# ScalarE asks for the first weights beside SyncE's first tile of x, and the zeros for the passes without data are cleared in two parts

## The chip, the cores and the metric

The kernel runs on one core of a Trainium2 chip. Its engines are TensorE (PE, with its weight loads shown apart as PEld), VectorE (DVE), ScalarE (ACT), GpSimd (POOL) and SyncE (SP); 16 DMA engines serve the core, and SP, ACT and POOL can ask for transfers. The metric is the time of one execution on the device in microseconds (us); the kernel before is given by the median of three runs.

## The reference

The input x has 2048 tokens of 576 features, in float32. Three things are computed from it and mixed:

```
g = _sigmoid((x * gate_w).sum(-1, keepdims=True))
a = _A_ref(x, A_w_r, A_w_i)        # irfft2( rfft2(x) * (w_r + 1j*w_i) )
b = _B_ref(x, B_w_gate, B_w_up, B_w_down)
                                   # h = _gelu(x @ w_gate) * (x @ w_up);  h @ w_down
return g * a + (1 - g) * b
```

w_gate and w_up are 576 by 4608, w_down is 4608 by 576. Most of the work is in these three products.

## The kernel before, in words

Every product is made at nearly full float32 precision out of several passes of TensorE: an operand is split into a high and a low part (tile names ending in hi and lo), and the high-high, high-low and low-high products are added. A pass is one MATMUL of a 128x128 block of weights with up to 512 columns.

The hidden layer has 36 blocks of 128 features, the tokens are cut into two halves (p), and each half into two tiles of 512 tokens (tb). All instructions are written in a fixed order, engine by engine (a manual schedule); an engine executes its own list in order, and semaphores connect the lists. The queues of SP, ACT and POOL issue their transfers in list order too.

The change is at the very start. Contraction over the 576 features is done in five steps k (KT = 5): k = 0 to 3 are 128 features each, k = 4 is the last 64, laid twice. `first_chains` (its passes are line 881) writes the first accumulations: for k = 0, 1, 2, then 4 and 3, the passes of hidden block 0 (into the PSUM tiles px) and of hidden block 1 (into pgu). For a step k it takes

- x0[k], a tile of x (a slice of `til`, 128 by 512, 256 KB), loaded by SP at line 1442 or 1446;
- w0[:, k] and w1[:, k], the weights of hidden blocks 0 and 1 (slices of `low`, 128 by 256, 128 KB each: gate and up), loaded by SP at lines 1444 and 1448 for k = 0 to 2, and by POOL at line 1470 for k = 4 and 3.

ACT makes the high part of the weights (line 240, tile gub) and DVE the low part (line 1477, also gub). The high part of x0[0] is made by DVE (a CAST, line 1476, tile xhi), later ones by ACT (line 240), and the low part by DVE (line 1481, tile xlo).

Before this data is there, TensorE runs passes without data: DVE clears a tile `idle` (a slice of the tile hb, line 1461), and six passes multiply zeros by zeros (line 1467). A small ACTIVATE on a cleared column (`warm`, a slice of gate, line 1464) brings ACT's table load to this time. POOL then clears 16 columns of `idle` (line 1468), which makes it wait for the end of the passes without data, and only then asks for its four slices of weights.

SP's semaphores for transfers go round in a ring of eight: the ninth transfer is issued when the first has landed, and so on.

Of the kernel before, what the change touches and what calls it, by code (L numbers as in the profile page):

```python
# [15 lines left out]
P = 128  # L16
# [9 lines left out]
TB = 512  # L26
# [123 lines left out]
def _block_of_token():  # L150

    out = [0] * 16
    for o in range(16):
        out[4 * LEFT[o % 4] + LEFT[o // 4]] = o
    return out, [4 * TAKEN[o % 4] + TAKEN[o // 4] for o in out]
# [20 lines left out]
def _build(nc, tc, a):  # L176
    with ExitStack() as ctx:
# [3 lines left out]
        vec, act, pl, pe = nc.vector, nc.scalar, nc.gpsimd, nc.tensor  # L181
# [4 lines left out]
        def f(x):  # L186
            return x.bitcast(F32)
# [7 lines left out]
        _, loc = _block_of_token()  # L195
# [28 lines left out]
        def ps_gu():  # L224
            return psum.tile([P, TB], F32, name="pgu", tag="pgu", bufs=2)
# [1212 lines left out]
        x0 = [til[i // 9][:, TB * (i % 9):TB * (i % 9 + 1)] for i in range(2 * KT)]  # L1438
        w0, w1 = (raw[j][:, 0:KT * 256].rearrange("p (t k) -> p t k", t=KT) for j in range(2))
        w0d, w1d = (a["wgu"][j].rearrange("p (t k) -> p t k", t=KT) for j in range(2))  # L1440
        for k in (0, 1, 2, 3):
            nc.sync.dma_start(x0[k], a["xt"][0][:, k, 0:TB])
            if k < 3:
                nc.sync.dma_start(w0[:, k], w0d[:, k])
            if k == 2:
                nc.sync.dma_start(x0[4], a["xt"][0][:, 4, 0:TB])
            if k < 3:
                nc.sync.dma_start(w1[:, k], w1d[:, k])
            if k == 2:
                nc.sync.dma_start(msk, a["msk"])  # L1450
# [7 lines left out]
        load_xs(0, 1, [tmp[:, D + TB * q:D + TB * (q + 1)] for q in range(4)])  # L1458

        idle = hb[2][:, 0]  # L1460
        vec.memset(f(idle), 0.0)
        warm = gate[:, 0:1]
        vec.memset(warm, 0.0)
        act.activation(warm, warm, AF.Gelu_apprx_tanh)
        ps = ps_gu()
        for _ in range(6):
            pe.matmul(ps, idle[:, 0:P], idle, start=True, stop=True)
        pl.memset(f(idle)[:, 0:16], 0.0)
        for w, wd, k in ((w0, w0d, 4), (w0, w0d, 3), (w1, w1d, 4), (w1, w1d, 3)):
            pl.dma_start(w[:, k], wd[:, k])  # L1470
# [163 lines left out]
```

## Time and profile before

| what | us |
|---|---|
| median of three runs | 1324.69 |
| lowest and highest of the three | 1323.77 and 1325.9 |
| the profiled execution, whole | 1325.16 |
| its span, first to last instruction | 1323.4 |
| what lies around the span (1325.16 - 1323.4) | 1.76 |
| PE busy in the span | 1317.2 |
| DVE busy | 1163.2 |
| ACT busy | 871.8 |
| POOL busy | 274.5 |

Times inside the execution are microseconds from the start of the span. Durations of instructions come from this one profiled execution. A busy engine is one that has an instruction in flight: matmuls are pipelined, so a PE that is always busy may still do its passes at different paces.

### The profile page before, as it was taken

How to read it: one execution, taken by the hardware profiler on the slowest of the kernel's cores; microseconds unless marked ns; L12 is line 12 of the kernel's file. 1: busy time of each engine (PE TensorE's matmuls, PEld its weight loads, DVE VectorE, ACT ScalarE, POOL GpSimd, SP SyncE). 2: the span in 40 equal slices, each digit the busy share in tenths (PEclk: the TensorE clock that was granted, in tenths of full speed). 3: DMA queues.
4: the chain of work that ended last, by engine and by line, in shares of the span. 5: the costliest groups of instructions: out<-in, count | busy, mean ns of one | idle time of the engine just before them, and what ended most of it. 6: DMA issues, size and time to landing. Idle time of an engine off the chain costs nothing.

```text
span 1323.4 us, 20232 instructions
## 1 busy us (share of the span) xinstructions
PE 1317.2 (100%) x7294; PEld 1166.3 (88%) x7294; DVE 1163.2 (88%) x1654; ACT 871.8 (66%) x1583; POOL 274.5 (21%) x347
## 2 busy tenths in 40 slices
PE   9999999999999999999999999999999999999998
PEld 7888888888888888888888898888888888888888
DVE  7789999978999997976889889799999879999854
ACT  5676765665657557787688888547675676676562
POOL 0011121221212212122302231211222242222331
PEclk9999999999999999999999999999999999999999
DMA  9346776797677777999989998787777897766897
GB/s 352 139 116 130 131 135 136 158 267 167 146 153 139 151 156 183 278 237 280 284 251 247 219 210 206 124 279 194 153 150 148 202 232 163 135 141 131 182 195 181
DMA packets 109221, 247.57 MB, mean 187 GB/s; under 512 B 12864, under 2 KB 18624, under 8 KB 107328
## 3 DMA queue, kind: packets, MB, share of 16 engines
q0 software_dynamic: 46560, 96.82, 45.2%
q1 hardware_dynamic: 62128, 149.01, 34.1%
q8 instruction: 57, 0.93, 0.3%
q10 hardware_dynamic: 432, 0.44, 0.1%
q14 instruction: 44, 0.36, 0.1%
HBM read 133.88 MB, written 109.95 MB: 184 GB/s over the span
## 4 chain that ended last, share of the span: by engine, by line
PE 96%; DVE 2%; DMA 1%; ACT 0%; issue 0%; SPq 0%; DVEq 0%; ACTq 0%
PE pdn L945 33%; PE pgu L1292 20%; PE px L1292 20%; PE pgu L1294 3%; PE px L1294 3%; PE pgu L861 3%; PE pgu L862 3%; PE pgu L863 3%; DMA til<-away 1%; PE pdn L305 1%; PE px L305 1%; PE px L861 1%; PE px L862 1%; PE px L863 1%; PE pgu L867 1%; PE pgu L868 1%
## 5 line engine op out<-in xcount | busy, mean ns | idle before, releaser
L958 POOL DMA_DIRECT2D yd<-stg x264 | 227.0, 865 | 937.7 <-ACT stg L977 864.3
L977 ACT ACTIVATE stg<-pdn,omg 128x576 f32<-128x576 f32 x276 | 204.4, 742 | 318.1 <-PE pdn L945 197.2
L945 PE MATMUL pdn<-dn,hb 128*128 128x288 f32 x1572 | 230.3, 294 | 0.0
L945 PEld LDWEIGHTS pdn<-dn,hb 128*128 128x128 f32 x1572 | 221.5, 188 | 8.9 <-ACT stg L977 0.4
L1279 DVE TENSOR_TENSOR gub<-low,gub 128x768 fp32r<-128x768 f32 x124 | 118.2, 954 | 9.7 <-ACT gub L1276 7.3
L1292 PE MATMUL pgu<-xhi,gub 128*128 128x512 f32 x392 | 121.6, 392 | 0.0
L240 ACT ACTIVATE gub<-low 128x512 fp32r<-128x512 f32 (+2 forms) x147 | 97.8, 666 | 23.0 <-DVE low L1269 14.5
L945 PEld LDWEIGHTS pdn<-dn,ext 128*128 128x128 f32 x672 | 100.8, 188 | 8.0
L1292 PE MATMUL pgu<-til,gub 128*128 128x512 f32 x420 | 107.5, 391 | 0.0
L945 PE MATMUL pdn<-dn,gub 128*128 128x288 f32 x672 | 106.5, 294 | 0.0
L945 PE MATMUL pdn<-dn,ext 128*128 128x288 f32 x672 | 106.5, 294 | 0.0
L945 PEld LDWEIGHTS pdn<-dn,gub 128*128 128x128 f32 x672 | 95.0, 188 | 0.0
L1292 PEld LDWEIGHTS pgu<-til,gub 128*128 128x128 f32 x420 | 76.9, 188 | 14.8 <-DVE gub L1279 0.3
L1292 PE MATMUL px<-xhi,gub 128*128 128x512 f32 x280 | 86.9, 391 | 0.0
L1292 PE MATMUL px<-til,gub 128*128 128x512 f32 x336 | 85.8, 391 | 0.0
L945 PE MATMUL pdn<-dn,hx 128*128 128x288 f32 x516 | 81.7, 294 | 0.0
L1292 PEld LDWEIGHTS pgu<-xhi,gub 128*128 128x128 f32 x392 | 70.9, 188 | 12.1
L1269 DVE TENSOR_TENSOR low<-low 128x768 f32<-128x768 f32 x81 | 77.2, 954 | 0.8
L1292 PE MATMUL pgu<-xlo,gub 128*128 128x512 f32 x196 | 76.4, 390 | 0.0
L862 PE MATMUL pgu<-xhi,gub 128*128 128x512 f32 x188 | 73.7, 392 | 0.0
L861 PE MATMUL pgu<-xhi,gub 128*128 128x512 f32 x188 | 73.7, 392 | 0.0
L863 PE MATMUL pgu<-xlo,gub 128*128 128x512 f32 x188 | 73.3, 390 | 0.0
(274 smaller groups left out, 2966.6 us busy)
## 6 DMA issues: line engine op xcount, KB each, us to landing
yd<-stg POOLq DMA_DIRECT2D x264, 288.0 KB, 5.0
low<-ws SPq DMA_DIRECT2D x94, 384.0 KB, 4.8
gub<-wd SPq DMA_DIRECT2D x56, 288.0 KB, 3.9
low<-wgu SPq DMA_DIRECT2D x13, 640.0 KB, 8.6
rows<-col POOLq DMA_DIRECT2D x32, 256.0 KB, 6.4
gub<-ws SPq DMA_DIRECT2D x18, 384.0 KB, 5.3
lo<-dn SPq DMA_DIRECT2D x18, 288.0 KB, 2.9
dn<-lo POOLq DMA_DIRECT2D x18, 288.0 KB, 5.4
```

The costliest lines, as they stand in the source:

```text
L240: act.activation(o, i, AF.Copy)
L305: pe.matmul(v[al][:, :NK], c[:, al, q], two(x)[:, al], start=n == 0, stop=n == 2)
L861: pe.matmul(ps, w[:, 0, k, c], xhi[tb][:, k], start=k == 0, stop=False)
L862: pe.matmul(ps, w[:, 1, k, c], xhi[tb][:, k], start=False, stop=False)
L863: pe.matmul(ps, w[:, 0, k, c], xlo[tb][:, k], start=False, stop=False)
L945: pe.matmul(ps[half], h[:, l, c], d[:, q, half * HD:(half + 1) * HD], start=part == 0 and n == 0, stop=part == 1 and n == 2)
L958: pl.dma_start(yd[u], o, accum_op=ALU.add)
L977: at(n, lambda: put(u, lambda o: act.activation(o.rearrange("p (c k) -> p c k", c=2), v[:, :, 0:HD], AF.Copy, scale=omg[:, u:u + 1]), i == 0))
L1269: vec.tensor_tensor(o, p, q, ALU.subtract)
L1279: vec.tensor_tensor(w[:, 0:5:2], x, f(w[:, 1:4]), ALU.subtract)
L1292: pe.matmul(ps, l, x[:, t], start=first and t == 0 and q == 0, stop=False, skip_group_check=True)
L1294: pe.matmul(ps, w[:, 512 + P * s:512 + P * (s + 1)], xt, start=False, stop=True, skip_group_check=True)
```

## The change

Two edits, both in the first lines that are written for the engines.

First, ACT is given a transfer: w0[:, 0], the weights of hidden block 0 for k = 0, which SP issued as its second transfer. It is now the first entry on ACT's list, ahead of the table load. SP's later transfers each move up by one place.

Second, the tile of zeros is cleared by two instructions, the first 128 columns and then the other 384, and the passes without data are two of 128 columns (on the part cleared first) and five of 512, in place of six of 512.

```
@@ -1438,9 +1438,10 @@
         w0d, w1d = (a["wgu"][j].rearrange("p (t k) -> p t k", t=KT) for j in range(2))
+        act.dma_start(w0[:, 0], w0d[:, 0])
         for k in (0, 1, 2, 3):
             nc.sync.dma_start(x0[k], a["xt"][0][:, k, 0:TB])
-            if k < 3:
+            if 0 < k < 3:
                 nc.sync.dma_start(w0[:, k], w0d[:, k])
             if k == 2:
                 nc.sync.dma_start(x0[4], a["xt"][0][:, 4, 0:TB])
@@ -1458,13 +1459,14 @@
         idle = hb[2][:, 0]
-        vec.memset(f(idle), 0.0)
+        vec.memset(f(idle[:, 0:P]), 0.0)
+        vec.memset(f(idle[:, P:]), 0.0)
         warm = gate[:, 0:1]
         vec.memset(warm, 0.0)
         act.activation(warm, warm, AF.Gelu_apprx_tanh)
         ps = ps_gu()
-        for _ in range(6):
-            pe.matmul(ps, idle[:, 0:P], idle, start=True, stop=True)
+        for n in (P, P, TB, TB, TB, TB, TB):
+            pe.matmul(ps[:, 0:n], idle[:, 0:P], idle[:, 0:n], start=True, stop=True)
```

Lines behind the first edit have a number one higher in the changed kernel, and two or more behind the second. Apart from these rows and the numbering, the lists of the five engines are the same in both kernels, and so are their waits, save that the two first transfers have changed semaphores.

SP's list at its start, before (til is x, low is weights, wgu and xt are the tensors in DRAM):

```order
L1442 DMA til_69<-xt 128x512
L1444 DMA low<-wgu 128x256
L1448 DMA low<-wgu 128x256
L1442 DMA til_69<-xt 128x512
L1444 DMA low<-wgu 128x256
L1448 DMA low<-wgu 128x256
```

and in the changed kernel:

```order
L1443 DMA til_69<-xt 128x512
L1449 DMA low<-wgu 128x256
L1443 DMA til_69<-xt 128x512
L1445 DMA low<-wgu 128x256
L1449 DMA low<-wgu 128x256
L1443 DMA til_69<-xt 128x512
```

The second entry is gone: w1[:, 0] now follows x0[0] at once, and all behind it stands one place earlier.

ACT's list at its start, before (gate is the cleared column, gub the split weights):

```order
L1464 ACT_TABLE_LOAD
L1464 ACTIVATE gate<-gate 128x1
L240 ACTIVATE gub_71<-low 128x256
L240 ACTIVATE gub_72<-low 128x256
L240 ACTIVATE gub_71<-low 128x256
```

and in the changed kernel:

```order
L1441 DMA low<-wgu 128x256
L1466 ACT_TABLE_LOAD
L1466 ACTIVATE gate<-gate 128x1
L240 ACTIVATE gub_71<-low 128x256
L240 ACTIVATE gub_72<-low 128x256
```

One transfer stands ahead of the table load; the rest of ACT's list has not moved.

PE's list at its start, before:

```order
L1467 MATMUL pgu<-hb_82 128x512 x6
L881 MATMUL px_220<-xhi_63,gub_71 128x512
L881 MATMUL px_221<-xhi_63,gub_71 128x512
L881 MATMUL px_220<-xhi_63,gub_71 128x512
L881 MATMUL px_221<-xhi_63,gub_71 128x512
```

and in the changed kernel:

```order
L1469 MATMUL pgu<-hb_82 128x128 x2
L1469 MATMUL pgu<-hb_82 128x512 x5
L881 MATMUL px_222<-xhi_63,gub_71 128x512
L881 MATMUL px_223<-xhi_63,gub_71 128x512
L881 MATMUL px_222<-xhi_63,gub_71 128x512
```

Only the passes without data differ: 2 x 128 + 5 x 512 = 2816 columns in place of 6 x 512 = 3072.

## Rows read from the trace of the kernel before

**Rows 1.** The page: busy time by engine, and the chain that ended last, by engine.

```profile
PE 1317.2 (100%) x7294; PEld 1166.3 (88%) x7294; DVE 1163.2 (88%) x1654; ACT 871.8 (66%) x1583; POOL 274.5 (21%) x347
...
PE 96%; DVE 2%; DMA 1%; ACT 0%; issue 0%; SPq 0%; DVEq 0%; ACTq 0%
```

**Rows 2.** Waits of PE, whole span: waited for, us in total, times, longest.

```profile
PE pgu L1467 <- DVE gate L1463: 1.5, 1, 1.5
PE px L305 <- DVE rows L293: 0.7, 1, 0.7
```

**Rows 3.** The chain that ended last, 0 to 20 us: start, us, what.

```profile
1.45 2.93 PE pgu L1467 x6
4.38 2.39 PE px L881 x6
6.77 1.39 PE pgu L881 x6
8.16 1.36 PE px L881 x6
```

**Rows 4.** Timeline of PE in short windows: start, us (of all in the row), passes.

```profile
1.45 0.80 PE L1467 MATMUL pgu<-hb 128*128 128x512 f32 x1 [1.45 <-DVE gate L1463]
...
3.75 0.63 PE L1467 MATMUL pgu<-hb 128*128 128x512 f32 x1
4.37 0.79 PE L881 MATMUL px<-xhi,gub 128*128 128x512 f32 x1
...
5.39 0.92 PE L881 MATMUL px<-xhi,gub 128*128 128x512 f32 x2
...
5.82 0.49 PE L881 MATMUL px<-xhi,gub 128*128 128x512 f32 x1
6.15 0.63 PE L881 MATMUL px<-xlo,gub 128*128 128x512 f32 x2
```

**Rows 5.** Timeline of DVE and ACT, 0 to 4.4 us: what leads to the passes.

```profile
0.73 1.28 ACT L1464 ACT_TABLE_LOAD   x1 [0.73 <-PEq L1620]
...
0.92 0.48 DVE L1461 MEMSET hb<- 128x512 f32 x1 [0.92 <-PEq L1620]
1.35 0.06 DVE L1463 MEMSET gate<- 128x1 f32 x1
...
2.03 0.20 ACT L1464 ACTIVATE gate<-gate 128x1 f32<-128x1 f32 x1
...
3.60 0.43 DVE L1476 CAST xhi<-til 128x512 fp32r<-128x512 f32 x1 [2.19 <-DMA til<-xt]
3.90 0.42 ACT L240 ACTIVATE gub<-low 128x256 fp32r<-128x256 f32 x1 [1.67 <-DMA low<-wgu]
```

**Rows 6.** Timeline of SP, 0 to 14 us: issue of its transfers.

```profile
0.74 0.38 SPq L1442 DMA_DIRECT2D til<-xt  x1
1.18 0.42 SPq L1444 DMA_DIRECT2D low<-wgu  x1
1.64 0.43 SPq L1448 DMA_DIRECT2D low<-wgu  x1
2.12 0.43 SPq L1442 DMA_DIRECT2D til<-xt  x1
...
6.21 0.33 SPq L1442 DMA_DIRECT2D til<-xt  x1
```

**Rows 7.** Line 1012, the output's stores: ACT's issue of a transfer, ns min/median/max.

```profile
L1012 ACTq DMA_DIRECT2D y<-stg x3: 338/339/374, 1317.6 to 1320.4; - x3
```

**Rows 8.** DMA traffic from 1.7 to 3.3, 3.3 to 4.8 and 4.8 to 6.8.

```profile
DMA packets 287, 0.40 MB, mean 248 GB/s; under 512 B 27, under 2 KB 159, under 8 KB 287
...
DMA packets 175, 0.20 MB, mean 132 GB/s; under 512 B 18, under 2 KB 139, under 8 KB 175
...
DMA packets 546, 0.71 MB, mean 353 GB/s; under 512 B 60, under 2 KB 342, under 8 KB 546
```

**Rows 9.** Timeline, 4 to 14 us: POOL's start, and two operands with the passes behind them.

```profile
4.50 2.33 POOL L1470 DMA_DIRECT2D low<-wgu x4
...
6.88 0.62 ACT L240 ACTIVATE xhi<-til 128x512 fp32r<-128x512 f32 x1
...
7.77 0.88 PEld L881 LDWEIGHTS px<-xhi,gub 128*128 128x128 f32 x4
...
12.27 0.75 DVE L245 SCALAR_TENSOR_TENSOR xtl<-xtl,msk,til 128x512 fp32r<-128x512 f32 x1
...
13.22 0.87 PEld L881 LDWEIGHTS px<-xtl,gub 128*128 128x128 f32 x4
```

More of the change, by code (lines that the diff above doesn't have):

```diff
@@ L1440, in _build @@
         w0d, w1d = (a["wgu"][j].rearrange("p (t k) -> p t k", t=KT) for j in range(2))
+        act.dma_start(w0[:, 0], w0d[:, 0])
         for k in (0, 1, 2, 3):
             nc.sync.dma_start(x0[k], a["xt"][0][:, k, 0:TB])
-            if k < 3:
+            if 0 < k < 3:
                 nc.sync.dma_start(w0[:, k], w0d[:, k])
@@ L1460, in _build @@
         idle = hb[2][:, 0]
-        vec.memset(f(idle), 0.0)
+        vec.memset(f(idle[:, 0:P]), 0.0)
+        vec.memset(f(idle[:, P:]), 0.0)
         warm = gate[:, 0:1]
@@ L1465, in _build @@
         ps = ps_gu()
-        for _ in range(6):
-            pe.matmul(ps, idle[:, 0:P], idle, start=True, stop=True)
+        for n in (P, P, TB, TB, TB, TB, TB):
+            pe.matmul(ps[:, 0:n], idle[:, 0:P], idle[:, 0:n], start=True, stop=True)
         pl.memset(f(idle)[:, 0:16], 0.0)
```

## The prediction

> **What bounds the kernel now.** I read the busy times and the chain on the page first, then PE's waits over the whole span, and then only the first 14 us, by the chain, the timeline of each engine and the DMA traffic. The page shows PE busy for 1317.2 of 1323.4 us and 96% of the chain on PE [rows 1]. PE's waits are two: 1.5 us until its first pass without data can start, and 0.7 us far behind, at a place that the change doesn't touch [rows 2]. So from the first pass on, PE is one dense stream, and a gain at the start is kept to the end as far as PE's stream really moves. Nothing later is tied to a fixed time: transfers are issued by lists and semaphores, which move with it.
>
> A busy PE isn't one at full pace. The chain shows the pace at the start: six passes without data in 2.93 us, the first six with data in 2.39 us, the next in 1.39 and then 1.36 us [rows 3]. 1.36 / 6 = 0.227 us for 512 columns, which is the level of 2.4 GHz (2.26 columns per ns). The early passes start 0.43 us apart (5.39 and 5.82), which is 1.2 GHz; between 5.82 and 6.15 the pace changes [rows 4]. I put the rise of the clock at 6.05, 4.6 us after the first pass at 1.45. Before the rise, a pass costs 0.20 us more than after it; an instant of work done there is worth 0.227 / 0.427 = 0.53 of an instant behind it.
>
> The first pass with data starts at 4.37 [rows 4]. It needs two things [rows 5]: the high part of x0[0], whose CAST starts as x lands, at 3.60, and ends at 4.03; and the high part of w0[:, 0], whose ACTIVATE starts as the weights land, at 3.90, and ends at 4.32. The weights are the later by 0.30 us, and PE starts 0.05 us behind them. The last pass without data starts at 3.75 and streams 0.43 us, to 4.18; PE's stream then has a hole of about 0.19 us.
>
> **The change part by part.** *The transfer on ACT.* SP issues x0[0] at 0.74 and w0[:, 0] at 1.18, w1[:, 0] at 1.64, and so on, 0.47 us apart [rows 6]. ACT is free at 0.73, where its table load starts [rows 5], so the weights are asked for 0.45 us earlier. The issue occupies ACT for 0.34 us, by its stores at the end [rows 7], to 0.43 us, by SP's first issues [rows 6]. The table load and the small ACTIVATE move back by that, from an end at 2.23 to 2.57 or 2.66; ACT then waits for the weights in any case, until 3.6 or so, and this costs nothing. It would cost only if the weights landed before 2.66, which is 1.9 us after the issue; the first transfer of SP took 2.86 (0.74 to 3.60).
>
> What it gives lies between two ends. Best: x0[0] lands as now, at 3.60, and the weights with it or before. Then the CAST ends at 4.03, PE starts at 4.08, 0.29 us earlier. Worst: the weights go ahead of x on all DMA engines and push it back. They are 128 KB, or 0.131 MB; at the 353 GB/s of a full stretch that is 0.37 us, at the 248 GB/s of the first stretch 0.53 us [rows 8]. x then lands at 3.97 to 4.13, and PE starts at 4.45 to 4.61: 0.08 to 0.24 us later than now. Without any overtaking, the bytes of both are moved by 3.88 already now, so the later of the two should come between 3.60 and 3.88; I take the middle, 3.74, and a first pass at 4.23, 0.14 us earlier.
>
> The Trainium skill (page "DMA: Bandwidth & Descriptors", section "Issuing engines are not separate DMA queues") says that transfers from several issuing engines run on the same 16 DMA engines and interleave, so that only the time of the issue is saved. By that rule the gain is at most the 0.45 us of the issue, and x pays for what the weights take. No row of the kernel before shows two such requests at once at the start, so the trace neither agrees nor disagrees. The sum by the row alone would be the best case, 0.29 us.
>
> SP's next transfers move up by 0.47 us each. That helps while the DMA engines have room, and the stretches to 4.8 have it (248 and 132 against 353 GB/s afterwards, [rows 8]); from 6.21 SP issues only as earlier transfers land [rows 6], and the rest of the start is bound by bytes, of which there are as many as before. What is late next: for k = 1 the high part of x is made at 6.88 to 7.50, and PE loads weights for its passes at 7.77 [rows 9], a margin of 0.27 us; the tail tile for k = 4 is ready at 13.02 and wanted at 13.22, a margin of 0.20 us [rows 9]. A PE that is 0.14 us earlier fits into both even if no transfer gains.
>
> *The zeros in two parts.* A 128x512 MEMSET takes 0.48 us and a 128x1 one 0.06 [rows 5]. By a line through both, 128 columns take 0.06 + 0.42 x 127 / 511 = 0.165 us and 384 columns 0.375 us. The first part ends at 0.92 + 0.165 = 1.085, and the first pass without data starts at about 1.13 instead of 1.45: 0.32 us earlier. The second part ends at about 1.42 to 1.46 (two MEMSETs overlap by 0.05 us: the second starts at 1.35, the first ends at 1.40), so the wide passes can go from 1.5. The two narrow passes take a quarter of 0.427 us each, 0.21 us, and 0.17 us for the first load of weights (the first pass took 0.80 against 0.63 us, [rows 4]): to 1.51. Five wide ones then stream until 1.51 + 5 x 0.427 = 3.65, 0.53 us earlier than the 4.18 of now. None of this is on the path to the first pass with data. It has two effects. POOL, which waits for these passes, asks for its four slices of weights at about 4.0 instead of 4.50 [rows 9]; they share the DMA engines with the transfers of k = 1 and 2, which are 0.47 us earlier too, so the order hardly changes, and I take nothing. And PE has been at work for longer, but has a hole of 4.23 - 3.65 = 0.58 us ahead of the first pass with data instead of 0.19.
>
> *The clock.* If it rises at 6.05 as now, the 0.14 us are gained at the slow pace and are worth 0.14 x 0.53 = 0.07 us. If the rise moves with the first pass, by 0.32 us, to 5.73, another 0.32 x 0.47 = 0.15 us come to it: 0.22 us. I take the middle, 0.15 us.
>
> **Sum.** 1325.16 (1323.4 of span and 1.76 around it) less 0.15 is 1325.01 for an execution like the profiled one. That one was 0.47 above the median of the three runs, so from the median the forecast is 1324.69 - 0.15 = 1324.54, told as 1324.5. The three runs alone spread over 2.1 us (1323.77 to 1325.9). A change under 0.2%, 2.65 us, is about what a measurement of this kernel can't tell from none, and this one is a twentieth of that.
>
> **Rivals.** *A, the forecast* (chance 0.55): between no gain and 0.3 us.
>
> *B, the transfers get in each other's way* (0.2): x lands up to 0.53 us later, the first pass starts at 4.45 to 4.61. By the same weight of 0.53 this loses 0.04 to 0.13 us: 1324.8. For it: CAST and ACTIVATE take equally long, so x0[0] has only 0.30 us to give before it is the later one. Against it: the DMA engines move 248 GB/s in that stretch, under the 353 of a full one, and the room would take most of the 0.131 MB.
>
> *C, the clock rises earlier than the first pass moves* (0.1). The bound is that all passes with data run at the full pace: those between 4.23 and 6.05 gain 1.82 x 0.47 = 0.86 us, and with the earlier start, now at its full value, 1.0 us: 1323.7. For it: the first pass is 0.32 us earlier; against it: fewer columns without data (2816 for 3072) and the larger hole.
>
> *D, the hole ahead of the first pass with data holds the clock down* (0.15), the rival on the slower side. The passes without data end at 3.65, and if what counts for the rise starts again with the data, the 4.6 us run from 4.23: the rise comes at 8.8, 2.8 us later than now. The price is 2.8 x 0.47 = 1.3 us: 1326.0. For it: the hole triples, to 0.58 us, and in case B it is 0.9. Against it: there is a hole already, and the pace rises all the same, 1.7 us behind it. It decides as soon as the rise comes later than 6.05 + 0.3 (0.14 us of gain at 0.47 us per us); over 0.2% it would be only if the rise came 5.6 us late.
>
> That the change doesn't do what it says I leave at nothing: the lists show the transfer on ACT and the seven passes, and whether it shows in the time is the forecast itself.
>
> **How the numbers follow.** The likeliest is A with 1324.5. The range has to take in C's 1323.7 and D's 1326.0 in part, and the scatter of a median of runs that spread over 2.1 us, for which I allow about 0.7 to each side of A and B; 1323.3 to 1325.9 leaves out most of D's upper half and C with a low scatter, together some 2 in 10. Faster by over 0.2% would want 2.65 us, more than twice C's bound: 0.03, for scatter. Slower by over 0.2% is D with a rise twice as late as I price it: 0.05. Within 0.2%: 0.92.
>
> **What would show it.** In the changed profile: ACT's queue has a transfer at about 0.73, and the table load starts at 1.1 to 1.2. The CAST of xhi starts between 3.6 and 3.9 and the first ACTIVATE of gub no later than 3.9; were either behind 3.95, B is right. PE's first pass without data starts at 1.1 to 1.2, the last ends near 3.65, the first with data starts at 4.1 to 4.35. The rise of the pace shows in the chain: the first six passes with data take under 2.39 us where the clock gains, over 2.5 where it loses, and D puts passes at 0.43 us into the second and third six. SP's third transfer starts at 1.64 instead of 2.12. From 14 us on, all rows should be those of before, moved by one amount. The prediction is wrong if that amount is over 0.5 us either way, or if PE shows a new wait between 6 and 14 us.

## The result, and the profile after

The changed kernel takes 1326.22 us (median of 22 runs, 1325.2 to 1328.05) against 1324.45 us for the kernel before (22 runs, 1323.76 to 1325.97): 1.77 us slower, a ratio of 1.0014 with a 95% interval of 1.0008 to 1.0019. That is within the 0.2% that I called no change, but it is a loss clear of the scatter, and outside the range, whose top was 1325.9.

The page and the waits of PE in the changed kernel, to be read against [rows 1] and [rows 2]:

```profile
PE 1318.3 (100%) x7295; PEld 1167.3 (88%) x7295; DVE 1163.1 (88%) x1655; ACT 871.9 (66%) x1583; POOL 274.0 (21%) x347
...
PE 99%; DMA 0%; DVE 0%; ACT 0%; DVEq 0%; issue 0%
```

```profile
PE pgu L1469 <- DVE hb L1462: 1.1, 1, 1.1
PE px L881 <- ACT gub L240: 0.7, 1, 0.7
```

PE starts 0.4 us earlier, as the second edit wants (1.1 us of waiting for the zeros instead of 1.5). A new wait of 0.7 us stands ahead of the first pass with data. The wait of 0.7 us far behind [rows 2] is gone; it is no part of the change (below).

The chain of the changed kernel from 0 to 20 us, to be read against [rows 3]:

```profile
0.73 3.41 DMA low<-wgu
4.14 0.02 issue
4.17 0.43 ACT gub L240
4.59 0.04 issue
4.64 2.93 PE px L881 x6
7.57 2.12 PE pgu L881 x6
9.68 1.39 PE px L881 x6
11.07 1.36 PE pgu L881 x6
```

The chain no longer goes over the passes without data, but over ACT's transfer: asked for at 0.73, it holds the weights until 4.17. The first pass with data starts at 4.64 instead of 4.37. The first six such passes take 2.93 us and the second six 2.12, where before they took 2.39 and 1.39: the pace of 0.43 us for 512 columns (1.2 GHz) lasts about 3 us longer. The third six start at 9.68 instead of 8.16, 1.52 us late, and the kernel keeps that.

The timeline of the changed kernel shows the cause of the late start, against [rows 5] and [rows 6]:

```profile
0.73 0.41 ACTq L1441 DMA_DIRECT2D low<-wgu  x1
...
0.74 0.39 SPq L1443 DMA_DIRECT2D til<-xt  x1
0.83 0.17 DVE L1462 MEMSET hb<- 128x128 f32 x1 [0.83 <-PEq L1622]
1.03 0.38 DVE L1463 MEMSET hb<- 128x384 f32 x1
...
1.05 2.93 PE L1469 MATMUL pgu<-hb 128*128 128x128 f32 x7 [1.05 <-DVE hb L1462]
1.17 1.28 ACT L1466 ACT_TABLE_LOAD   x1 [1.17 <-PEq L1622]
...
3.95 0.43 DVE L1478 CAST xhi<-til 128x512 fp32r<-128x512 f32 x1 [2.53 <-DMA til<-xt]
...
4.17 0.72 ACT L240 ACTIVATE gub<-low 128x256 fp32r<-128x256 f32 x2 [1.49 <-DMA low<-wgu]
```

The request is made 0.45 us earlier, and both tiles land later: x at 3.95 instead of 3.60, the weights at 4.17 instead of 3.90.

The traffic from 1.7 to 3.3 us says why, against the first of [rows 8] (q1 is SP's queue, q10 ACT's; the figures of a queue are packets, MB, and the share of the time of the 16 DMA engines that its packets took):

```profile
DMA packets 254, 0.38 MB, mean 237 GB/s; under 512 B 9, under 2 KB 129, under 8 KB 254
...
q1 hardware_dynamic: 142, 0.27, 62.4%
q10 hardware_dynamic: 112, 0.11, 22.2%
```

In the kernel before, the same stretch has SP's queue alone:

```profile
q1 hardware_dynamic: 287, 0.40, 78.5%
```

Two queues are served at once, packet beside packet, and together they move 237 GB/s, no more than SP's queue alone did (248). Before, SP's packets already took 78.5% of the engines' time, and now the two queues take 84.6%: there was less room than the GB/s suggest. So the tile x pays for the weights, and the weights wait among the packets of x. The Trainium skill (page "DMA: Bandwidth & Descriptors", section "Issuing engines are not separate DMA queues") says that transfers started by different engines interleave on the same DMA engines, and that only the time of the issue is saved. The trace agrees on the interleaving; of the issue time nothing was saved here, since the weights, asked for 0.45 us earlier, landed 0.27 us later.

### The profile page after: what moved, and what is told of

It is laid out like the page before. It is cut to its first block, busy times and chain, and to the rows that moved or that the text cites. A ratio compares the mean times of both kernels' runs of the same rounds, so it can differ in the third digit from the quotient of the medians.

```text
span 1324.0 us, 20235 instructions
## 1 busy us (share of the span) xinstructions
PE 1318.3 (100%) x7295; PEld 1167.3 (88%) x7295; DVE 1163.1 (88%) x1655; ACT 871.9 (66%) x1583; POOL 274.0 (21%) x347
## 4 chain that ended last, share of the span: by engine, by line
PE 99%; DMA 0%; DVE 0%; ACT 0%; DVEq 0%; issue 0%
PE pdn L945 34%; PE pgu L1292 20%; PE px L1292 20%; PE pgu L1294 3%; PE px L1294 3%; PE pgu L861 3%; PE pgu L862 3%; PE pgu L863 3%; PE pdn L305 1%; PE px L305 1%; PE px L861 1%; PE px L862 1%; PE px L863 1%; PE pgu L867 1%; PE pgu L868 1%; PE px L881 1%
```

## The experiments

The trace records the instant at which the granted clock rises. The views print a granted clock of 1.00 from the start of the span, since that record holds nothing ahead of the rise; the pace of the passes agrees with the record (in the changed kernel 0.43 us apart up to 9.05, 0.23 behind it). The table gives, for each kernel and from its profiled execution, when the stream of passes without data ends (start of the last one and 0.43 us), when the first pass with data starts, the hole between the two, and the rise. The last column compares medians with the kernel before on the same chip. The ratio beside it is estimated from all runs together, so it need not have the sign of the difference of the medians.

| kernel | stream ends | first data | hole | rise | median less before's, us (ratio, interval) |
|---|---|---|---|---|---|
| before | 4.18 | 4.37 | 0.19 | 6.02 | |
| before, again | 4.18 | 4.34 | 0.16 | 5.05 | |
| changed | 3.79 | 4.64 | 0.85 | 9.01 | +1.77 (1.0014, 1.0008 to 1.0019) |
| changed, again | 3.78 | 4.89 | 1.11 | 7.84 | |
| transfer alone | 4.18 | 4.74 | 0.56 | 7.61 | -0.17 (1.0003, 0.9994 to 1.0012) |
| zeros alone | 3.78 | 4.26 | 0.48 | 7.00 | +0.06 (1.0003, 0.9994 to 1.0011) |
| before, five passes | 3.76 | 4.33 | 0.57 | 8.33 | +0.15 (1.0003, 0.9993 to 1.0012) |
| before, four passes | 3.33 | 4.29 | 0.96 | 8.20 | +0.94 (1.0006, 0.9997 to 1.0015) |
| transfer, five passes | 3.75 | 4.62 | 0.87 | 9.73 | +1.81 (1.0012, 1.0003 to 1.0021) |
| changed, six wide | 4.21 | 4.62 | 0.41 | 6.82 | +0.41 (1.0002, 0.9993 to 1.0011) |
| changed, seven wide | 4.64 | 4.70 | 0.06 | 5.74 | -0.54 (0.9999, 0.9991 to 1.0008) |
| zeros, six wide | 4.21 | 4.21 | 0 | 4.72 | +0.02 (0.9999, 0.9991 to 1.0008) |
| before, seven passes | 4.61 | 4.60 | 0 | 6.48 | +0.16 (1.0001, 0.9992 to 1.0009) |
| changed, transfer later | 3.78 | 4.66 | 0.88 | 10.03 | +2.17 (1.0018, 1.0009 to 1.0027) |
| transfer, five passes late | 5.07 | 5.07 | 0 | 6.98 | +0.71 (1.0006, 0.9997 to 1.0015) |
| before, four passes late | 4.65 | 4.64 | 0 | 5.96 | +0.86 (1.0005, 0.9996 to 1.0013) |

The profiled execution is one of the runs that the median is taken from, and not always a typical one: that of the transfer alone took 1325.2 us (median 1324.45), that of the four passes late 1324.21, the least of its eleven.

A first batch takes the edits apart.

**The transfer alone.**

```
+        act.dma_start(w0[:, 0], w0d[:, 0])
...
-            if k < 3:
+            if 0 < k < 3:
```

> The first edit alone: ACT asks for the weights of k = 0, but the zeros are cleared at once and six passes of 512 columns run without data, as before. Theory H (the hole in PE's stream ahead of the first pass with data decides when the clock rises, the transfer only widens it): the six passes end their stream at 4.2 us, the first pass with data starts at 4.6, a hole of 0.45 us, between 0.19 before and 0.9 after; some of the loss, 1324.7 to 1325.8 us. Theory T (the two requests at once delay the data, and that is the loss, through PE's order of work): the whole loss, 1326.2. Theory Z (the zeros and their fewer columns are the loss): 1324.6, the 0.1 us of the later data alone.

Measured 1324.45 against 1324.62 us, no loss in the median, though two of the eleven runs took 1326.39 and 1327.89. The data is as late as in the changed kernel (first pass with data at 4.74), so theory T, by which the late data is the whole loss, falls.

**The zeros alone.**

```
-        vec.memset(f(idle), 0.0)
+        vec.memset(f(idle[:, 0:P]), 0.0)
+        vec.memset(f(idle[:, P:]), 0.0)
...
-        for _ in range(6):
-            pe.matmul(ps, idle[:, 0:P], idle, start=True, stop=True)
+        for n in (P, P, TB, TB, TB, TB, TB):
+            pe.matmul(ps[:, 0:n], idle[:, 0:P], idle[:, 0:n], start=True, stop=True)
```

> The second edit alone: zeros cleared in two parts, two passes of 128 and five of 512 columns without data, SP asks for all transfers as before. The passes end their stream at 3.65 to 3.75 us, the first pass with data starts at 4.37, a hole of 0.65 us. Theory H: most of the loss, 1325.3 to 1326.0. Theory T: no loss, 1324.3 to 1324.6. Theory Z: the whole loss, 1326.1.

Measured 1324.68 against 1324.62, no loss either, so theory Z falls; and H (the hole decides), which gave each edit a part of the loss, isn't borne out by the medians: two edits that cost 0.06 us or less apart cost 1.77 together. This is shown for the medians only. The intervals of the two, from eleven runs each, reach up to 1.6 and 1.5 us, and in the two profiles the rise is later than before (7.61 and 7.00).

**The changed kernel with two more passes without data**, which fill the hole.

```
-        for n in (P, P, TB, TB, TB, TB, TB):
+        for n in (P, P, TB, TB, TB, TB, TB, TB, TB):
```

> The changed kernel with two more passes of 512 columns without data (two of 128 and seven of 512), so that their stream ends at 4.6 us, where the first pass with data starts. Theory H: the clock rises at about 6 us again and only 0.1 us of the later data is left: 1324.3 to 1324.8. Theory T: the data is as late as in the changed kernel, 1326.2. Theory Z leaves it at 1324.5 too, since the columns without data are more.

Measured 1324.08 against 1324.62: the loss is gone, with both edits in and the data as late as before this addition. Its chain:

```profile
1.06 3.78 PE pgu L1469 x9
4.84 1.99 PE px L881 x6
6.83 1.37 PE pgu L881 x6
8.20 1.36 PE px L881 x6
```

The second six passes with data run at the full pace, and the third six start at 8.20, where the changed kernel has 9.68.

**The kernel before with five passes instead of six** (`range(5)`).

> The kernel before with five passes of 512 columns without data instead of six; transfers and zeros as before. Their stream ends at 3.75 us, the first pass with data starts at 4.37: a hole of 0.6 us with the transfers of before. Theory H: a loss of about that of the second edit alone, 1325.3 to 1326.0. Theory T: 1324.4, no loss, and POOL's earlier request for its weights costs nothing. Theory Z: 2560 columns instead of 3072, the whole loss or more, 1326.2.

Measured 1324.77 against 1324.62; H expected 0.7 us and more. Up to here a hole of 0.5 to 0.6 us is harmless in the medians and one of 0.85 isn't. The second batch puts this to the test.

**The changed kernel with one more pass of 512**: (P, P, and six TB).

> The changed kernel with one more pass of 512 columns without data (two of 128 and six of 512). Their stream ends at about 4.2 us, the first pass with data starts at 4.65 to 4.7: a hole of 0.45 us, half that of the changed kernel, with its transfers as they are. Theory H (the hole of 0.85 us keeps the clock down, the two edits are harmless alone because each leaves 0.5 to 0.6): no loss, 1324.1 to 1324.7. Theory L (late data and narrow passes together keep it down, whatever the hole): near 1326.

Measured 1324.72 against 1324.31, at the top of what H expects, 1.4 us under the loss of the changed kernel in its own comparison.

**The transfer with five passes**: two changes without a cost put together, without the second edit.

```
+        act.dma_start(w0[:, 0], w0d[:, 0])
...
-        for _ in range(6):
+        for _ in range(5):
```

> The first edit with five passes of 512 columns without data; zeros cleared at once. Two changes that each cost nothing alone (0.0 and 0.1 us) are put together without the second edit. The stream without data ends at 3.76 us, the first pass with data starts at 4.65 to 4.75: a hole of 0.9 to 1.0 us. Theory H: the loss of the changed kernel, 1325.9 to 1326.6. Theory A (the costs add): 1324.7. Theory L (narrow passes needed): 1324.7.

Measured 1326.12 against 1324.31: +1.81 us, the whole loss. Theory A, by which costs add, expected 1324.7 and falls, and so does L: the narrow passes are not needed. The chain repeats that of the changed kernel:

```profile
4.62 2.93 PE px L881 x6
7.54 2.45 PE pgu L881 x6
9.99 1.39 PE px L881 x6
```

**The kernel before with four passes** (`range(4)`): neither edit is made.

> The kernel before with four passes of 512 columns without data; all transfers and the zeros as before, neither edit made. Their stream ends at 3.33 us, the first pass with data starts at 4.35: a hole of 1.0 us. Theory H: a loss of 1.2 to 1.8 us, 1325.8 to 1326.4, with the data as early as before. Theory L (the transfer on ACT is needed for the loss): 1324.7 to 1325.0.

Measured 1325.25 against 1324.31: +0.94 us, under what H expects (1.2 to 1.8) and over L's; its interval reaches 0.9997, so it settles nothing by itself.

**The zeros in two parts with one more pass of 512**: (P, P, and six TB), all transfers by SP.

> The second edit with one more pass of 512 columns without data (two of 128 and six of 512), SP asks for all transfers as before. The stream without data runs from 1.1 to 4.2 us, the first pass with data starts at 4.3: a hole of 0.1 us. Theory H: the clock rises before 6 us in most executions and the data is as early as before; 1323.8 to 1324.3, the fastest so far, under the kernel before by 0.3 to 0.6 us. Theory L: 1324.5, as before.

Measured 1324.33 against 1324.31. H expected a gain (1323.8 to 1324.3). The clock rose at 4.72 in its profile, the earliest of all, and the median did not follow; the kernel before, run again, shows where that goes (below).

**The kernel before with seven passes** (`range(7)`).

> The kernel before with seven passes of 512 columns without data instead of six. The stream runs from 1.45 to 4.6 us and has no hole; the first pass with data, which could start at 4.37, is held up to 4.6. Theory H: the rise no longer depends on the hole, and the delay of 0.25 us costs 0.13 us or less; 1324.0 to 1324.5, the kernel before or a little under it. If more work without data always helped, however late, it would be under 1324.0; if the held-up passes cost their full time, 1324.7.

Measured 1324.5 against 1324.34: no difference. Here, with no hole left, more work without data gained nothing.

**The changed kernel with ACT's request behind its small ACTIVATE** in the list.

```
-        act.dma_start(w0[:, 0], w0d[:, 0])
...
         act.activation(warm, warm, AF.Gelu_apprx_tanh)
+        act.dma_start(w0[:, 0], w0d[:, 0])
```

> The changed kernel with ACT's request for the weights behind its table load and its small ACTIVATE, at about 2.25 us instead of 0.73, when the tile x0 is already moving. If x0 was late in the changed kernel because the two requests shared the DMA engines from the start, the CAST of x starts at 3.6 again (3.95 with the request at 0.73). If x0 was late for another reason (SP's later transfers each being one place earlier), it stays at 3.9 or later. The weights land at 4.5 to 5.0 in either case, the first pass with data starts at 5.0 to 5.5 with a hole of 1.2 us or more, and theory H expects a loss of 1.9 to 2.4 us, 1326.3 to 1326.9.

The request went out at 1.47, before the ACTIVATE had run, and x was in time again:

```profile
1.47 0.38 ACTq L1466 DMA_DIRECT2D low<-wgu  x1
...
3.51 0.43 DVE L1478 CAST xhi<-til 128x512 fp32r<-128x512 f32 x1 [2.09 <-DMA til<-xt]
...
4.19 0.72 ACT L240 ACTIVATE gub<-low 128x256 fp32r<-128x256 f32 x2 [1.96 <-DMA low<-wgu]
```

So x0 was late because the two requests started together. All 16 profiles bear this out: the CAST of x starts at 3.93 to 4.24 in the seven where ACT asks at 0.73, and at 3.42 to 3.61 in the nine others. The weights, asked for 0.74 us later than in the changed kernel, land at the same time (4.19 and 4.17): the early request gave nothing. The hole is that of the changed kernel, and the loss too: 1326.51 against 1324.34.

**Both kernels once more**, for one profile each.

> The changed kernel once more, one profile, to see how far the rise of the clock wanders from execution to execution: with the first pass with data at 4.6 to 4.75 the rise should again come after 8 us if the hole is what holds it (9.0 in the first profile), and the first 24 passes with data should end 1 to 2 us behind the kernel before; a rise near 6 us would mean that 9.0 was chance.

The rise came at 7.84, before the 8 us that I expected, although the first pass with data, at 4.89, and the hole, of 1.11 us, came out larger than in the first profile; the third six passes start at 9.28:

```profile
4.89 2.93 PE px L881 x6
7.82 1.46 PE pgu L881 x6
9.28 1.36 PE px L881 x6
```

> The kernel before once more, one profile: the rise between 5 and 7.5 us (6.0 in the first profile), and no wait of PE for its rows near 690 us if that wait of 0.7 us in the first profile was a matter of one execution.

The rise came at 5.05, and the late wait is not there. PE shows one wait in all:

```profile
PE pgu L1467 <- DVE gate L1463: 1.5, 1, 1.5
```

In this execution the chain of the start is no longer PE's:

```profile
4.97 5.53 DMA low<-wgu
10.50 0.02 issue
10.52 0.73 ACT gub L240 x2
11.25 0.52 ACT xtl L240
...
12.90 0.32 ACT gub L240
13.22 0.00 issue
13.22 2.55 PE px L881 x10
```

After an early rise PE catches up with the transfers of k = 2 and with what ACT makes behind them, the tail tile and the last weights; I had given the tail tile a margin of 0.20 us. A gain at the start is cut there. In the profile with the rise at 4.72 it is cut sooner, at the second and third six passes, which wait for their weights and for x of k = 1:

```profile
6.08 1.53 PE pgu L881 x6
7.61 1.54 PE px L881 x6
9.15 1.36 PE pgu L881 x6
```

That is why this early rise brought little in its own execution. When the clock rose in the other runs of that kernel isn't known.

One rival was open: fewer passes had always come with a larger hole. Two kernels keep the few passes and move them up against the data, by clearing the zeros three times over.

```
-        vec.memset(f(idle), 0.0)
+        for _ in range(3):
+            vec.memset(f(idle), 0.0)
```

> The first edit with five passes of 512 columns without data (1.8 us slower than before), but their start put off by 0.9 us: DVE clears the zeros three times over, so that the same five passes stream from 2.3 to 4.6 us, up to the first pass with data. PE does the same work ahead of the data, later, without a hole. Theory H (the hole decides): most of the loss is gone; the rise can come later than before by the later start, up to 0.9 us or 0.4 us of time: 1324.3 to 1325.1. Theory W (the work done ahead of the data decides, or the time since PE began): the loss stays or grows, 1326.0 to 1326.8.

Measured 1325.03 against 1324.32: of the 1.81 us of the same five passes without the delay, 0.71 are left. The three MEMSETs took longer than I had priced, so the passes started at 2.77 and pushed the first pass with data from 4.62 to 5.07; even so the kernel gained 1.1 us. Theory W, by which the work ahead of the data or the time since PE began decides, expected 1326 or more and falls here.

> The kernel before with four passes of 512 columns without data (0.9 us slower than before), their start put off by 0.9 us in the same way: they stream from 2.3 to 4.2 us, with a hole of 0.1 to 0.2 us ahead of the data at 4.3 to 4.4, in place of 0.96. Theory H: 1324.3 to 1325.0, under the four passes that start early. Theory W: 1325.3 to 1326.

Measured 1325.18 against 1324.32: +0.86, where the four early passes cost +0.94. This lies between the theories, above H's 1325.0 and below W's 1325.3. Closing this hole cost PE 1.3 us of earlier work and 0.3 us of a later first pass with data, and nothing was won in the median. The profile doesn't explain this median: its rise is at 5.96, but it is of the fastest execution.

## Why the prediction was wrong

**The path and its prices were right.** PE is the bound, and what happens at the start is kept: from the start of the 41st pass with data (14 to 16 us) to the end of the span, the thirteen profiles without a late wait of PE take 1308.06 to 1308.14 us. The zeros in two parts did nearly what was worked out: 0.17 and 0.38 us for the two MEMSETs (0.165 and 0.375 worked out), the first pass 0.4 us earlier (0.32), the end of the stream at 3.79 (3.65). The price of the clock held: 0.47 us for each us by which the rise is later, and 0.53 for each us by which the first pass with data is later. For the changed kernel that is 0.47 x (9.01 - 6.02) + 0.53 x (4.64 - 4.37) = 1.55 us, and the third six passes are 1.52 late; for the transfer with five passes it is 0.47 x 3.71 + 0.53 x 0.25 = 1.88, and they are 9.99 - 8.16 = 1.83 late. In all ten profiles of altered kernels that have a hole, the 41st pass with data is late against the first profile of before by this sum, to within 0.04 us.

**The first failed step is the middle that I took for the first pass with data, 4.23.** It rested on the sentence that without any overtaking the bytes of both are moved by 3.88, and on the room that I read from the GB/s. That left out that SP's next transfers move up too and share the engines (when the last packet of the weights starts, at 3.57, SP's queue has started 0.35 MB, 0.09 more than x holds), and that the engines were 78.5% taken already: the stretch moved 237 GB/s with two queues and 248 with one. Measured: 4.64, just past the far end of rival B (4.45 to 4.61). At an unchanged rise this alone would cost 0.14 us.

**The second, and the one that carries the loss, is the term of the clock.** The sum put the rise between 5.73 and 6.05, a gain, and left the hole to rival D. The runs showed 9.01 (7.84 in the second profile): 0.47 x 2.99 = 1.4 us lost in the place of 0.15 gained. B and D had chances of their own, 0.2 and 0.15, but they are one chain: the late data widens the hole (0.85 us, not the 0.58 of the forecast), and the hole goes with the late rise. D worked out on B's start, 4.61 + 4.6 = 9.2 for the rise, gives 0.47 x 3.15 + 0.13 = 1.6 us, near the measured 1.77; D as I priced it, on A's start, gave 1.3, and the range was cut on the side where both meet. That the 4.6 us come so near is in part luck: in the four profiles of kernels that lost 1.77 us or more, the rise came 2.95 to 5.37 us behind the first pass with data.

**What is shown, and what is open.** Shown: in the profiles the time lost is the later rise and the later first pass with data, but for the late waits of PE in three of them; in the medians neither edit has a loss alone, and together they cost 1.77 us; the same loss comes without the second edit when the hole is as large (+1.81); it goes, or most of it, when the hole is filled (-0.54 and +0.41 in the changed kernel, +0.71 for five passes moved up). Not shown: what exactly decides the rise. In the profiles it comes later with larger holes up to 0.88 us (6.82 to 8.33 for 0.41 to 0.57, 9.01 to 10.03 for 0.85 to 0.88), but holes of 0.96 and 1.11 went with 8.20 and 7.84. The four early passes lost half of what their hole of 0.96 us should cost, and the four late ones as much without one. The time since PE's start and the amount of work may count as well; these runs do not separate them. No version is faster than the kernel before beyond its interval; the best, 0.54 us lower, has an interval of 0.9991 to 1.0008.

## What to carry to other kernels

Here a second queue brought no data earlier, because the first requests already took most of the DMA engines' time: look at that share and not only at the GB/s, ask in the order in which the data is needed, and watch what the first tile pays. When work without data is to keep TensorE going, look at where it ends and not only at where it starts; an edit that ends it earlier and an edit that brings the data later widen the same gap, and here they cost nothing in the median one by one, and 1.77 us together. When two rivals in a forecast touch the same gap, price them together.

## What the runs showed of the hardware that I had not expected

The rise of the clock wanders from execution to execution of one kernel: 6.02 and 5.05 us in two profiles of the kernel before, 9.01 and 7.84 in two of the changed one. At 0.47 us for each us the first pair differs by 0.46 us, of the 2.2 us over which the runs of before spread. One profile of such a start says little about the median: the transfer alone had a rise at 7.61 in its profile and no loss in the median of 11 runs.

A profiled execution can hold a wait of its own. The first profile of the kernel before lost 0.9 us near 680 us, mostly in the wait of 0.7 us for the tile rows [rows 2], which is in none of the other profiles; without it the spans of the two kernels would differ by about 1.5 us, not by 0.6 (1324.0 and 1323.4). Two other profiles, of kernels that lost 1.8 us and more, have such a wait elsewhere; how often the runs without a profile have one isn't known. The waits of PE for the transfer with five passes:

```profile
PE pgu L1468 <- DVE gate L1464: 1.5, 1, 1.5
PE pgu L861 <- ACT gl L902: 1.1, 1, 1.1
PE px L881 <- ACT gub L240: 0.7, 1, 0.7
```
